# Four first columns of q and k through the SyncE and ScalarE queues instead of three

## The chip, the cores and the metric

The kernel runs on one core of one Trainium2 chip. Its time is the device time of one execution in microseconds (us); the median of five runs is given. The engines are PE (matmul, with PEld for its weight loads), DVE (vector), ACT (scalar), POOL and SP. Transfers between memory (HBM) and the core's SBUF go through 16 DMA engines, which serve several queues: SP and ACT each issue into a hardware queue (in the profile q1 and q10), POOL into a software queue (q0). A transfer in POOL's queue can convert fp32 to bf16 on its way; one in the other two keeps the type.

## What is computed

A cross-covariance attention is followed by a mixture of adapters. With B = 4 batches, N = 6400 rows and C = 256 channels:

```python
def _attn_ref(q, k, v, tau):
    qn = q / (np.linalg.norm(q, axis=1, keepdims=True) + 1e-06)
    kn = k / (np.linalg.norm(k, axis=1, keepdims=True) + 1e-06)
    s = kn.transpose(0, 2, 1) @ qn / tau
    s = s - s.max(-1, keepdims=True)
    a = np.exp(s)
    a /= a.sum(-1, keepdims=True) + 1e-09
    return v @ a

def _moe_ref(x, w_gate, A, B):          # x: the attention's output, 25600 x 256; 8 experts of rank 16, the best 2 of each row
    topk = np.argpartition(-(x @ w_gate), 2, axis=1)[:, :2]
    ...
    delta[mask] += w[mask, k, None] * ((x[mask] @ A[e]) @ B[e])
    ...
    return x + delta
```

The inputs q, k and v are fp32, 26.2 MB each; the output is fp32, 26.2 MB. For the first step of each batch, all of q and k has to pass through the 256 x 256 product before any row of v can be used.

## The kernel before

**Tiles.** The 6400 rows of a batch are split over 128 partitions, so that each partition holds 50 neighbouring rows. One such row on all partitions is called a column: 128 x 256 elements, 128 KB in fp32, contiguous within a partition. A batch has `NC` = 50 columns. q and k are loaded in pieces of 17, 17 and 16 columns (`QK`, L215) into bf16 tiles named `qk`, v in five pieces of 10 columns (`V`). For each column, step `G` (L571 to L589) multiplies k by q into the PSUM tile `acc` (L577, two matmuls of 256 columns), and, where the squared norms are not taken elsewhere, k by k (L581) and q by q (L586). For the column groups listed in `OFF` the squares are made on ACT (L599) and added up on DVE (L605) instead, so `G` has only its two matmuls there. Group 0, which is columns 0 to 5 of batch 0, is in `OFF` for q and for k.

**Order.** A planner written in Python (`Plan`, L69) simulates the engines with estimated costs, a model of PE's clock and a model of the DMA queues, and lists all steps in the order in which they would start. The program is then written out in that order; each engine works its own instructions strictly in this order, and waits where data is not there yet. Where the planner expects PE to be idle it can put filler matmuls (`warm`, L761), which write to an otherwise unused bank. POOL issues the loads of q, k and v in the planner's order (L562). At most eight of them are out at a time in the planner's model. SP issues the stores of the output (L912); some of these wait for a later load by way of a tiny transfer (`hold`, L629).

**The start.** For batch 0 the first piece of q and of k is loaded in two parts: `PARTS[(0, 0)]` is `((0, 2), (2, 15))`. The first part does not go through POOL. SP loads it for q and ACT for k, as fp32, into one scratch tile (`W["first"]`, in the buffer of the output tile y0, room for 10 columns), and these two instructions are moved ahead of everything else in the program (`first_ahead`, L428). ACT then casts each to bf16 into the `qk` tile (`do_cast`, L757). How many columns this first part holds is not taken from `PARTS` but from the constant `FIRST`, 3 here; POOL's load of the second part begins behind it:

```python
            if (b, c) == (0, 0):
                n = FIRST
                ...
                lo = "qk".index(what) * n
                W[what] = W["first"][:, lo:lo + n, :]
                early.append((nc.sync if what == "q" else nc.scalar).dma_start(W[what], src[b, :, 0:n, :]))
                return
        if (what, b, i) in (("q", 0, 0), ("k", 0, 0)):
            c, n = FIRST, c + n - FIRST
        nc.gpsimd.dma_start(t[:, c - c0:c - c0 + n, :], src[b, :, c:c + n, :])
```

The planner does not read `FIRST`. Behind the two first loads SP and ACT load the small constants (expert matrices and gate, L492 to L496), which DVE copies at 34.4 us (L538). The remaining pieces of q and k for batch 0 follow in POOL's queue, then the rest in the order of `WORDS`.

Of the kernel before, what the change touches and what calls it, by code (L numbers as in the profile page):

```python
# [32 lines left out]
class Clock:  # L33


    WINDOW, FIRST, LOW, HIGH = 3.413, 0.31, 0.5, 0.8

# [3 lines left out]
    def at(self, t):  # L41
        w = max(0, int((t - self.FIRST) / self.WINDOW) + 1)
        while len(self.cold) <= w:
            share = self.busy[-1] / self.WINDOW
            self.cold.append(share < (self.HIGH if self.cold[-1] else self.LOW))
            self.busy.append(0.0)
        return w

    def took(self, t, us):

        end, w = t, self.at(t)
        while us > 1e-9:
            pace = 2.0 if self.cold[w] else 1.0
            step = min(us * pace, max(self.FIRST + w * self.WINDOW - end, 1e-6))
            self.busy[w] += step
# [5 lines left out]
    def idle(self, t):  # L61

        w = self.at(t)
        return t - self.FIRST - (w - 1) * self.WINDOW - self.busy[w] > self.SPARE

# [347 lines left out]
PARTS = {(0, 0): ((0, 2), (2, 15)), (0, 2): ((34, 8), (42, 5), (47, 3)), (3, 2): ((34, 8), (42, 5),  # L413
        (47, 3))}
FINE = 2
FIRST = 3
OFF = {(0, 0, 'k'), (0, 0, 'q'), (0, 1, 'q'), (0, 2, 'k'), (0, 2, 'q'), (0, 4, 'q'), (0, 5, 'q'),
        (0, 6, 'k'), (0, 6, 'q'), (0, 7, 'k'), (0, 8, 'q'), (1, 0, 'k'), (1, 0, 'q'), (1, 1, 'q'),
        (1, 2, 'k'), (1, 5, 'q'), (1, 6, 'k'), (1, 7, 'k'), (1, 7, 'q'), (1, 8, 'q'), (2, 0, 'q'),
# [23 lines left out]
def kernel(  # L443
# [101 lines left out]
    def do_load(s, what, b, i, c, n):  # L545
        if what == "v":
            t, src, c0 = sb(s, "v", (b, i), [P, PC * max(n for _, n in V), C], BF16), v_v, c
        else:
            t = sb(s, "qk", (what, b, i), [P, max(n for _, n in QK), C], BF16)
            src, c0 = {"q": q_v, "k": k_v}[what], QK[i][0]  # L550
            if (b, c) == (0, 0):
                n = FIRST
                if "first" not in W:
# [6 lines left out]
# [3 lines that stand above are left out]
# [407 lines left out]
```

## Time and profile before

| | us |
|---|---|
| median of five runs | 255.23 (255.10 to 255.43) |
| the profiled execution, whole | 255.7 |
| its span, from the first to the last instruction | 253.9 |
| PE sees its first matmul | 5.6 |
| POOL's first load of q issued, landed | 1.4, 10.3 |
| POOL's first load of k issued, landed | 2.1, 14.6 |
| the last loads end, about | 223 |
| the last store issued, landed | 245.9, 253.0 |

The profile is a page about one execution. Its parts that are used here: the busy time of each engine; the span in 40 equal slices, where each digit is a busy share in tenths; the DMA queues with packets, MB and their time as a share of 16 engines; and the chain that ended last, followed back from the last instruction to whatever released each step. The trace behind it can be asked for instructions in order of time (start, duration, engine, line, operation, tile, shapes, and in brackets the idle time before it with what ended it), and for sums over chosen stretches. MB and GB/s count bytes as they are written: a transfer of POOL's that converts reads twice as many as are shown.

### The profile page before, as it was taken

What the parts mean: (1) busy time and instruction counts of PE and PEld (TensorE: products, weight loads), DVE (VectorE), ACT (ScalarE), POOL (GpSimd) and SP (SyncE); (2) the same over time, 40 slices, a digit from 0 to 9 for tenths busy, and PEclk for the clock granted to TensorE, in tenths of its full rate; (3) what the DMA queues carried; (4) which work ended last, traced back from release to release, by engine and by line L of the source; (5) the groups of instructions that cost most, each with busy time, mean ns of one, the idle gap of its engine ahead of it and who ended that gap; (6) DMA issues with size and microseconds to landing.
All of it is one profiled execution on the core that took longest, in us unless ns stands there. A gap on an engine that the chain in (4) does not pass through costs nothing.

```text
span 253.9 us, 5843 instructions
## 1 busy us (share of the span) xinstructions
PE 218.3 (86%) x2343; PEld 193.0 (76%) x2343; DVE 193.1 (76%) x527; ACT 149.5 (59%) x270; POOL 29.9 (12%) x58
## 2 busy tenths in 40 slices
PE   1165984899999998999999999989999989999960
PEld 0053962698989996799889989779999869999950
DVE  0055589779989987898999994689888889888810
ACT  4354437447767554877667538443766747557760
POOL 7001220040020002000030100510000200000000
PEclk9999997599999999999999999999999999999996
DMA  8999999999999999999999999999999999999994
GB/s 220 209 218 209 210 219 212 215 221 213 218 213 212 313 293 296 260 214 216 214 217 219 213 216 219 211 209 346 283 286 318 333 326 313 324 416 434 423 410 176
DMA packets 11819, 66.57 MB, mean 262 GB/s; under 512 B 1424, under 2 KB 2320, under 8 KB 7184
## 3 DMA queue, kind: packets, MB, share of 16 engines
q0 software_dynamic: 7488, 38.93, 74.7%
q1 hardware_dynamic: 3968, 26.74, 25.9%
q10 hardware_dynamic: 336, 0.53, 0.6%
q8 instruction: 18, 0.29, 0.4%
q14 instruction: 9, 0.07, 0.1%
HBM read 78.91 MB, written 26.21 MB: 414 GB/s over the span
## 4 chain that ended last, share of the span: by engine, by line
PE 53%; DMA 36%; DVE 3%; ACT 2%; POOL 1%; issue 1%; POOLq 0%; ACTq 0%
DMA qk<-in_k_dram 28%; PE Y_ps L899 13%; PE acc L577 9%; DMA qk<-in_q_dram 9%; PE T_ps L772 6%; PE Y_ps L904 6%; PE ZL_ps L796 4%; PE gzT_ps L886 4%; PE acc L586 2%; PE acc L581 2%; PE Z_ps L863 2%; DVE a_bf L747 2%; ACT a_exp L699 1%; PE log_ps L810 1%; POOL qk L562 1%
## 5 line engine op out<-in xcount | busy, mean ns | idle before, releaser
L577 PE MATMUL acc<-qk 128*128 128x256 bf16 x400 | 71.3, 286 | 18.7 <-DMA qk<-in_k_dram 12.5
L605 DVE TENSOR_TENSOR ssq<-ssq,sq 128x1280 f32<-128x1280 f32 (+1 forms) x27 | 43.4, 1606 | 23.2 <-ACT sq L599 21.1
L899 PE MATMUL Y_ps<-a_bf,vT 128*128 128x256 bf16 x400 | 60.0, 273 | 0.0
L753 ACT COPY y<-Y_ps 128x512 f32<-128x512 f32 x79 | 45.9, 586 | 18.3 <-PE Y_ps L904 15.6
L577 PEld LDWEIGHTS <-qk 128*128 128x128 bf16 x400 | 34.8, 102 | 23.9 <-DMA qk<-in_k_dram 15.2
L599 ACT ACTIVATE sq<-qk 128x1280 f32<-128x1280 bf16 (+1 forms) x27 | 36.9, 1366 | 26.6 <-DVE ssq L605 19.7
L899 PEld LDWEIGHTS <-vT 128*128 128x128 bf16 x400 | 38.9, 98 | 4.0
L904 PE MATMUL Y_ps<-ball,gzT 128*128 128x256 bf16 x200 | 38.2, 273 | 0.3 <-DVE gzT L755 0.3
L581 PE MATMUL acc<-qk 128*128 128x128 bf16 x242 | 34.4, 224 | 0.0
L772 PE MATMUL T_ps<-ident,v 128*128 128x128 f32 x200 | 27.3, 279 | 0.1
L562 POOL DMA_DIRECT2D v<-in_v_dram x20 | 12.1, 606 | 128.4 <-PE T_ps L772 81.0
L581 PEld LDWEIGHTS <-qk 128*128 128x128 bf16 x242 | 24.3, 100 | 3.4
L753 ACT COPY vT<-T_ps 128x512 f32<-128x512 f32 (+1 forms) x44 | 21.7, 515 | 8.2 <-PE T_ps L772 7.9
L874 DVE TENSOR_TENSOR gz<-zl,gateg 128x256 bf16<-128x256 f32 x70 | 26.0, 444 | 0.3
L772 PEld LDWEIGHTS T_ps<-ident,v 128*128 128x128 f32 x200 | 22.9, 145 | 1.1 <-issue 0.8
L586 PE MATMUL acc<-qk 128*128 128x128 bf16 x168 | 23.0, 218 | 0.0
L904 PEld LDWEIGHTS <-gzT 128*128 128x128 bf16 x200 | 19.4, 98 | 3.0 <-DVE gzT L755 0.6
L796 PE MATMUL ZL_ps<-waA_sb,vT 128*128 128x136 bf16 x280 | 19.7, 222 | 1.1 <-DVE waA_sb L741 0.9
L886 PE MATMUL gzT_ps<-ident,gz 128*128 128x128 f32 x100 | 20.4, 278 | 0.0
L796 PEld LDWEIGHTS <-vT 128*128 128x128 bf16 x280 | 17.8, 98 | 1.8 <-issue 1.5
L755 DVE COPY gzT<-gzT_ps 128x256 f32<-128x256 f32 (+1 forms) x39 | 14.9, 390 | 4.1 <-PE gzT_ps L886 3.6
L599 ACT ACTIVATE ssq<-qk 128x1536 f32<-128x1536 bf16 x8 | 11.9, 1483 | 10.1 <-DMA qk<-in_q_dram 5.3
(80 smaller groups left out, 271.0 us busy)
## 6 DMA issues: line engine op xcount, KB each, us to landing
out_dram<-y SPq DMA_DIRECT2D x18, 1280.0 KB, 17.9
v<-in_v_dram POOLq DMA_DIRECT2D x20, 640.0 KB, 20.3
qk<-in_q_dram POOLq DMA_DIRECT2D x7, 1088.0 KB, 23.5
qk<-in_k_dram POOLq DMA_DIRECT2D x7, 1088.0 KB, 28.2
qk<-in_q_dram POOLq DMA_DIRECT2D x2, 1024.0 KB, 18.1
qk<-in_k_dram POOLq DMA_DIRECT2D x2, 1024.0 KB, 22.4
out_dram<-y SPq DMA_DIRECT2D x4, 512.0 KB, 7.5
qk<-in_q_dram POOLq DMA_DIRECT2D x2, 512.0 KB, 17.1
```

The lines of the kernel that those rows point to most:

```text
L577: nc.tensor.matmul(acc[ic][:, 0:256], kt[:, j, ic::CC], qt[:, j, :], start=c == 0, stop=False, skip_group_check=True)
L581: nc.tensor.matmul(acc[ic][:, 256:384], kt[:, j, ic::CC], kt[:, j, ic::CC], start=False, stop=False, skip_group_check=True)
L586: nc.tensor.matmul(acc[ic][:, 384:512], qt[:, j, ic * P:(ic + 1) * P], qt[:, j, ic * P:(ic + 1) * P], start=False, stop=c == NC - 1, skip_ ...
L599: nc.scalar.activation(out[:, 0:n, :], t[:, j:j + n, :], ACT.Square)
L605: nc.vector.tensor_tensor(out=t, in0=t, in1=held["sq", (w, b, g), ""][:, 0:n, :], op=OP.add)
L753: nc.scalar.copy(out, in_)
L772: nc.tensor.matmul(ps[:, j, :], vt[:, c + j, :].bitcast(FP32), W["ident32"], is_transpose=True, start=(j == 0), stop=(j == n - 1))
L796: nc.tensor.matmul(ps[:, j, :], vT_of(b, i, c + j)[:, :, ic], st[b]["waA"][:, ic, :], start=(j == 0 and ic == 0), stop=(j == n - 1 and ic ...
L874: nc.vector.tensor_tensor(out=pairs[:, h].rearrange("p c (e r) -> p c e r", e=E), in0=z[:, 2 * h:2 * h + 2, :].rearrange("p c (e r) -> p c ...
L886: nc.tensor.matmul(ps[:, j, :], pairs[:, j * P:(j + 1) * P], W["ident32"], is_transpose=True, start=(j == 0), stop=(j == n // 2 - 1))
L899: nc.tensor.matmul(ps[:, j, :], vT_of(b, i, c + j)[:, :, ic], st[b]["a"][:, ic, :], start=(j == 0 and ic == 0), stop=False, skip_group_che ...
L904: nc.tensor.matmul(ps[:, j, :], pair[:, :, j], W["B"], start=False, stop=(j == 1), skip_group_check=True)
```

## The change

One constant changes. SP's load of q and ACT's load of k at the start take four columns instead of three (512 KB each instead of 384), the two casts on ACT take 1024 elements per partition instead of 768, and POOL's first load of q and of k begin at column 4 and take 13 columns instead of 14 (832 KB of fp32 instead of 896). The scratch tile then holds 8 columns of its 10. The planner's result, and with it the number and order of instructions on every engine, is the same.

```diff
 PARTS = {(0, 0): ((0, 2), (2, 15)), (0, 2): ((34, 8), (42, 5), (47, 3)), (3, 2): ((34, 8), (42, 5),
         (47, 3))}
 FINE = 2
-FIRST = 3
+FIRST = 4
```

## The prediction

> **What bounds the kernel now.** I read the page's busy shares and 40 slices first, then the DMA queues, then the chain that ended last, then the start and the end closely.
>
> ```profile
> PE 218.3 (86%) x2343; PEld 193.0 (76%) x2343; DVE 193.1 (76%) x527; ACT 149.5 (59%) x270; POOL 29.9 (12%) x58
> ...
> DMA  8999999999999999999999999999999999999994
> ...
> q0 software_dynamic: 7488, 38.93, 74.7%
> q1 hardware_dynamic: 3968, 26.74, 25.9%
> ...
> HBM read 78.91 MB, written 26.21 MB: 414 GB/s over the span
> ```
>
> PE is the busiest engine, but the row to look at is DMA: 9 in every slice between the first and the last. The two big queues took 74.7% and 25.9% of the time of 16 engines, together the whole span. So the transfers are the bound, and the total is bytes over rate: 105.1 MB at 414 GB/s are 253.9 us, the span. This does not depend on PE's small waits as long as no queue runs dry.
>
> ```profile
> 3.69 21.22 DMA qk<-in_k_dram
> 24.91 0.28 issue
> 25.19 21.10 DMA qk<-in_k_dram
> 46.33 2.32 PE acc L577 x10
> ```
>
> These are lines of the chain that ended last, in order of time: up to 46.33 us it is two loads of 21 us each. Their issue took 0.5 us; the rest was spent in the queue behind other loads. A load that is issued 0.3 us later lands no later.
>
> **The change, part by part.** The instruction orders of the two kernels are the same on all engines; only the sizes of six differ: the two first loads, their two casts, and the two Pool loads behind them, which shrink from 14 columns to 13 (896 to 832 KB).
>
> (a) *The extra column on SP's and ACT's queues.* While the hardware queue of k ran alone, and while the software queue ran alone, the DMA view has:
>
> ```profile
> q10 hardware_dynamic: 69, 0.21, 104.4%
> ...
> q0 software_dynamic: 242, 1.62, 100.1%
> ```
>
> The first line is from 3.0 to 3.5 us: 69 packets of 3072 bytes, full engines, 0.21 MB in 0.5 us, 424 GB/s of fp32. The second is from 5 to 13 us: 1.62 MB written as bf16 in 8 us, 203 GB/s, which are 405 GB/s of fp32 read. One column of one tensor is 128 KB of fp32. By the hardware queue it takes 0.131 MB / 424 GB/s = 0.31 us, by the software queue 0.131 / 405 = 0.32 us. Two columns are added to the one (+0.62 us) and taken from the other (-0.65 us). The sum is -0.03 us, below what these rows resolve. I take 0.
>
> (b) *Whether the bytes cost the same at the very start.* The stretches show start and end, length, busy times of PE, PEld, DVE, ACT, POOL, granted clock, DMA share and GB/s:
>
> ```profile
> 0.90:1.40 0.50, 0.00 (x0) 0.00 (x0) 0.00 (x0) 0.00 (x0) 0.00 (x0) 1.00 0.78 129
> 1.40:1.90 0.50, 0.00 (x0) 0.00 (x0) 0.00 (x0) 0.09 (x1) 0.48 (x1) 1.00 1.18 154
> 1.90:2.40 0.50, 0.00 (x0) 0.00 (x0) 0.00 (x0) 0.50 (x1) 0.50 (x2) 1.00 0.69 215
> 2.40:2.90 0.50, 0.00 (x0) 0.00 (x0) 0.00 (x0) 0.50 (x1) 0.42 (x2) 1.00 0.95 375
> ```
>
> From 0.90 to 2.40 us only (129 + 154 + 215) x 0.5 = 0.249 MB moved, where 424 GB/s would have needed 0.59 us: 0.91 us are lost. If the slow part costs by packet and not by byte, a 4096-byte packet carries a third more in it, and the bytes added are free. All 0.26 MB free would be -0.65 us, the lower bound. If the loss grows with the size of q's first load, it is 0.91 x 1/3 = +0.30 us, the upper bound. The trace cannot tell which. From 2.40 us on the rate is near full, and most of the extra bytes move there, so I take 0, and keep -0.65 and +0.30.
>
> (c) *What becomes later at the start, and its cover.* q's and k's first loads were issued at 0.00 and 0.12 us and landed 3.5 and 4.6 us later, at 3.5 and 4.7: with 0.31 us for each column ahead of them they become 3.8 and 5.3. A cast of 768 elements took 0.82 us; two lengths of the squares (1.25 us for 1280 elements, 1.48 for 1536) give 0.23 us for 256 more, so 1.05 us. The two casts end at 6.4 instead of 5.54 us, and PE begins there. On PE, 6 matmuls took 1.46 us at the start; 8 take 1.95, until 8.4 us. On ACT the next instruction behind the casts is:
>
> ```profile
> 10.44 1.48 ACT L599 ACTIVATE ssq<-qk 128x1536 f32<-128x1536 bf16 x1 [4.90 <-DMA qk<-in_q_dram]
> ...
> 14.65 1.89 PE L577 MATMUL acc<-qk 128*128 128x256 bf16 x8 [7.60 <-DMA qk<-in_k_dram]
> ```
>
> ACT sat idle 4.90 us before its next work and PE 7.60 us, so 0.9 us more of casts costs nothing. Without this cover it would be 0.9 us.
>
> The constants behind these loads on the SP and ACT queues land 0.6 us later than at 5.6 us; the copies on DVE that read them begin at 34.4 us. Pool's q load (issued at 1.42, 8.9 us to landing, so 10.3) lands 0.62 later by the hardware bytes ahead of it and 0.32 earlier by its own: at 10.6 us. Pool's k load (2.07 and 12.5) stays at 14.6. So ACT's squares at 10.44 move to 10.75, their DVE add from 13.32 to 13.6, and Pool's ninth load, which waits for q's landing, is issued at 10.9 instead of 10.63. That load landed 24 us after its issue: its place in the queue is kept. All of these have their next wait at 14.6 us or later, on something unmoved.
>
> (d) *What PE is spared behind k's landing.* Column 3 now runs in the idle time before 14.65 us: 2 matmuls of 0.236 us. Its 14 columns become 13, and PE's next wait, for the load that lands at 24.91, begins earlier. Nothing is gained; PE waits longer. This touches the clock:
>
> ```profile
> 20.40:23.82 3.42, 1.58 (x11) 0.89 (x9) 1.87 (x2) 1.48 (x1) 0.53 (x1) 1.00 1.01 211
> ...
> 37.47:40.88 3.41, 1.00 (x8) 0.71 (x8) 3.31 (x13) 1.90 (x3) 0.00 (x0) 1.00 1.06 222
> 40.88:44.30 3.42, 1.96 (x6) 0.53 (x4) 3.32 (x5) 2.86 (x2) 0.00 (x0) 0.50 1.00 209
> ```
>
> The stretches are cut at the times at which the granted clock changed. After 1.00 us of PE work in 3.41 us the clock was halved (at 40.88); after 1.58 us it was kept (at 23.82). The 0.47 us spared are of slow matmuls (the clock became full only at 20.40, where they halve), so the 1.58 become 1.58 - 0.24 = 1.34 us, between the two. I take the clock as kept, and price the other case as a rival.
>
> The Trainium skill, TensorE: Matmul & The Clock Gate, Part 1, speaks against the change in one point: it says PE falls back to half its clock after at least one idle window of some 3.4 us, and the wait before 24.95 us grows from 2.98 to 3.2 us. By that rule the clock would be kept, for no window is wholly idle, and the edit costs 0. But the rows above show a halving after a window with 1.00 us of work in it, so here the measurement decides and the case stays open.
>
> **Sum.** Own time of the profiled execution: 255.7 us, 253.9 of span and 1.8 around it. Bytes 0, start 0 (-0.65 to +0.30), casts 0, PE 0. The median, 255.23, is 0.47 under that execution; the forecast stands on the median: 255.2 us. The likeliest case has 254.8 to 255.6.
>
> **Rivals.**
>
> *1. The start gives something (faster).* The added bytes ride in the slow 1.5 us for free. For it: q's packets there were few and slow with nothing else in the queues. Against: 0.249 of q's 0.39 MB had moved by its end; the rest and k's come later at full rate. Whole, -0.65: 254.6 us; it shows where Pool's first k load lands, now 14.6 us.
>
> *2. PE's clock falls at 23.82 us (slower).* Place: PE works from 24.95 to 30.64 us; at half clock it gets through half of the 5.69 us, so 2.85 us of work are left over, until a full window wakes it at 30.64. Cover: PE's waits behind it, 0.67 us before 34.09 and 2.41 before 39.93, together 3.08. It decides from the point where the work in the window falls under a bound somewhere between 1.00 and 1.58 us, and it costs only if column 49 then comes late for the norms on DVE and ACT (39.8 us) and if that reaches a load's issue. Price: 0 with the cover, 2.85 without, 258.1. I take 1.0, for part of the cover lies before the end of the columns: 256.2 us. Against it: loads wait 17 us and more in the queue, so PE's lateness hardly reaches the DMA engines.
>
> *3. PE wakes one window earlier (faster).* In 44.30 to 47.71 us PE worked 2.70 of 3.41 us and stayed at half clock. If the k load at 46.3 lands 0.1 us earlier, this is 2.8. Waking at 47.71 instead of 51.12 spares half of 3.41, 1.7 us: 253.5 us if PE bound the rest. It does not: the last store was issued at 245.90 and landed 7.1 us later, behind other stores, so PE's end is covered.
>
> *4. The change does nothing, since the planner costs none of it.* The sizes in the instruction orders exclude it; what remains is that it moves no time, which is the forecast.
>
> **How the numbers follow.** What a measurement can tell from no change is about 0.2%, 0.5 us. Chances: forecast 0.62 (same 0.85 of it, the rest halved: 0.53 same, 0.045 to each side); rival 1 0.13 (0.12 faster); rival 2 0.18 (0.16 slower, 0.02 same); rival 3 0.07 (0.06 faster). Faster 0.22, same 0.55, slower 0.23 with the rounding. The range reaches to the foot of rival 1, 254.5, and to the price taken for rival 2, 256.1.
>
> **What would show it.** Right: the first loads land 0.3 and 0.6 us later, Pool's first k load at 14.6 +- 0.2, DMA at 9 from slice 2 to 39, the same MB in all queues but 0.26 MB more in SP's and ACT's and 0.13 less in Pool's, and a halved clock only from 40.9 to 51.1 us. Step (b) is wrong if Pool's k load lands at under 14.3 or over 14.8; (c) if ACT's squares or PE wait for a cast after 10 us; (d) if the clock is halved at 23.8 us. The forecast as a whole is wrong if a DMA slice between falls under 9, or if the landings of the middle loads have moved by other than those of the first.

## The result and the profile after

The changed kernel took 254.80 us (median of 21 runs, 254.69 to 255.36) beside 255.41 us for the kernel before (39 runs, 255.08 to 255.91). The ratio is 0.9979, with a 95% interval of 0.9973 to 0.9985: 0.54 us faster, 0.38 to 0.69. This is just over the 0.2% that counted as a change, and inside the range, but it is not the forecast's 255.2 with no change.

The page of the changed kernel shows the same DMA-bound picture, with the bytes moved between the queues as foreseen:

```profile
span 253.1 us, 5843 instructions
...
DMA  9999999999999999999999999999999999999995
...
q0 software_dynamic: 7488, 38.80, 74.6%
q1 hardware_dynamic: 3968, 26.87, 26.1%
q10 hardware_dynamic: 336, 0.66, 0.8%
```

POOL's queue wrote 0.13 MB less of bf16 (0.26 of fp32 less to read), SP's and ACT's 0.13 MB more each. The DMA digits differ in the first slice, 9 for 8, and in the last, 5 for 4. The span is 0.8 us shorter, more than the medians differ: the profiled execution before took 255.7 us, 0.3 over its median of the 39 runs, and the one after took 254.87, 0.07 over its median.

The start in order of time (start, length, engine, line, in brackets the idle time before and what ended it):

```profile
4.14 1.04 ACT L758 CAST qk<-y 128x1024 bf16<-128x1024 f32 x1 [0.31 <-DMA y<-in_q_dram]
...
5.44 1.04 ACT L758 CAST qk<-y 128x1024 bf16<-128x1024 f32 x1 [0.26 <-DMA y<-in_k_dram]
...
6.54 1.89 PE L577 MATMUL acc<-qk 128*128 128x256 bf16 x8 [6.54 <-ACT qk L758]
...
10.04 1.48 ACT L599 ACTIVATE ssq<-qk 128x1536 f32<-128x1536 bf16 x1 [3.56 <-DMA qk<-in_q_dram]
...
13.95 1.46 PE L577 MATMUL acc<-qk 128*128 128x256 bf16 x6 [5.52 <-DMA qk<-in_k_dram]
```

Everything fed by SP and ACT comes later, everything fed by POOL earlier. The casts are 0.22 us longer and end 0.94 us later, and PE runs 8 matmuls for 6 at once, in time it has to spare. But the squares on ACT begin at 10.04 instead of 10.44, and PE's wait for POOL's k load ends at 13.95 instead of 14.65 us. From this second shift on the two traces keep a distance: POOL's next loads of 1088 KB take 15.9 and 20.5 us to their landing instead of 16.6 and 21.2. The chain that ended last, in order of time, goes through other loads, but has the same shape:

```profile
4.73 24.43 DMA qk<-in_k_dram
29.15 0.28 issue
29.44 21.93 DMA v<-in_v_dram
51.36 0.04 issue
51.41 0.67 PE T_ps L772 x4
```

It reaches PE's work only at 51 us, again by two loads whose time is spent in the queue, not in their issue.

### The profile page after: what moved, and what is told of

Read it like the earlier page. It is cut to its first block, busy times and chain, and to the rows that moved or that the text cites. A ratio compares the mean times of both kernels' runs of the same rounds, so it can differ in the third digit from the quotient of the medians.

```text
span 253.1 us, 5843 instructions
## 1 busy us (share of the span) xinstructions
PE 217.1 (86%) x2343; PEld 192.3 (76%) x2343; DVE 193.0 (76%) x527; ACT 150.5 (59%) x270; POOL 29.9 (12%) x58
## 4 chain that ended last, share of the span: by engine, by line
PE 50%; DMA 38%; DVE 4%; ACT 2%; POOL 2%; issue 1%; ACTq 0%; POOLq 0%
DMA qk<-in_k_dram 21%; PE Y_ps L899 13%; DMA v<-in_v_dram 9%; DMA qk<-in_q_dram 9%; PE acc L577 8%; PE Y_ps L904 6%; PE T_ps L772 6%; PE ZL_ps L796 4%; PE gzT_ps L886 4%; PE acc L586 2%; PE acc L581 2%; PE Z_ps L863 2%; DVE a_bf L747 2%; ACT a_exp L699 1%; PE log_ps L810 1%; POOL qk L562 1%
## 5 line engine op out<-in xcount | busy, mean ns | idle before, releaser
L599 ACT ACTIVATE sq<-qk 128x1280 f32<-128x1280 bf16 (+1 forms) x27 | 36.9, 1365 | 27.2 <-DVE ssq L605 19.7
L581 PE MATMUL acc<-qk 128*128 128x128 bf16 x242 | 34.7, 225 | 0.0
L772 PEld LDWEIGHTS T_ps<-ident,v 128*128 128x128 f32 x200 | 22.0, 141 | 2.8 <-DMA v<-in_v_dram 0.9
L586 PE MATMUL acc<-qk 128*128 128x128 bf16 x168 | 23.6, 223 | 0.0
L755 DVE COPY y<-Y_ps 128x512 f32<-128x512 f32 x21 | 14.3, 689 | 3.4 <-PE Y_ps L904 3.1
```

Of the source, the lines that this page charges most:

```text
L581: nc.tensor.matmul(acc[ic][:, 256:384], kt[:, j, ic::CC], kt[:, j, ic::CC], start=False, stop=False, skip_group_check=True)
L586: nc.tensor.matmul(acc[ic][:, 384:512], qt[:, j, ic * P:(ic + 1) * P], qt[:, j, ic * P:(ic + 1) * P], start=False, stop=c == NC - 1, skip_ ...
L599: nc.scalar.activation(out[:, 0:n, :], t[:, j:j + n, :], ACT.Square)
L755: nc.vector.tensor_copy(out, in_)
L772: nc.tensor.matmul(ps[:, j, :], vt[:, c + j, :].bitcast(FP32), W["ident32"], is_transpose=True, start=(j == 0), stop=(j == n - 1))
```

## The experiments

Three theories were set up. A: at the start the DMA engines get less done than later, and bytes that ride there are free. B: the gain is PE's, which has column 3 behind it early. C: a chance of the layout, the execution or PE's clock windows. D (POOL's packets come too early) and E (the constants' small packets should run beside POOL's and not alone) came up on the way. One quantity is compared throughout: the HBM traffic of the first 12.5 us, which is the MB of q1 and q10 plus twice those of q0 (POOL's queue writes half of what it reads). The DMA view of that stretch, before:

```profile
q0 software_dynamic: 243, 1.63, 66.0%
q1 hardware_dynamic: 416, 0.52, 17.7%
q10 hardware_dynamic: 336, 0.53, 12.9%
```

and after:

```profile
q0 software_dynamic: 252, 1.57, 60.9%
q1 hardware_dynamic: 416, 0.66, 19.8%
q10 hardware_dynamic: 336, 0.66, 16.0%
```

These are 4.31 and 4.46 MB. The rate later is about 0.43 MB a us (215 GB/s written by POOL's queue from 7.5 to 12.5 us before, twice that read), so 0.15 MB are 0.35 us; two traces of one kernel differ by 0.04 to 0.06 MB in it.

**Column 3 loaded twice** (`twice`):

```diff
-                n = FIRST
+                n = FIRST + 1
 ...
-        nc.scalar.copy(held["qk", (what, 0, 0), ""][:, 0:FIRST, :], W[what])
+        nc.scalar.copy(held["qk", (what, 0, 0), ""][:, 0:FIRST, :], W[what][:, 0:FIRST, :])
```

> SP and ACT load four columns, POOL still loads fourteen: column 3 of q and of k is loaded twice (once into the scratch tile, where nobody reads it), 0.26 MB of fp32 more in all. Theory A (the DMA engines are underfed in the first 6 us, and bytes that ride there are free): 0 to +0.15 us against before (ratio 1.000 to 1.0006), POOL's first k load lands at 14.5 to 14.8 us. Theory B (the gain is PE's, which has column 3 behind it before k lands, and bytes cost the same everywhere): +0.6 us, ratio 1.0024, landing at 15.2 us, and no gain from the four columns since PE still waits for POOL's part. Theory C (a chance of the program's layout or of PE's clock windows): no relation, within 0.5 us.

Measured: 255.33 against 255.25 us, ratio 1.0002 (0.9994 to 1.0011); POOL's first k load was issued at 2.1 us and took 12.5, so it landed at 14.6. 4.52 MB in 12.5 us, 4.26 without the bytes loaded twice:

```profile
q0 software_dynamic: 239, 1.60, 61.5%
q1 hardware_dynamic: 416, 0.66, 19.3%
q10 hardware_dynamic: 336, 0.66, 14.9%
...
qk<-in_k_dram POOLq DMA_DIRECT2D x1, 896.0 KB, 12.5
```

The added 0.26 MB, 0.6 us by the rate later, cost at most 0.3. A holds; B, which charged 0.6 us, falls.

**Column 3 not loaded** (`skip`):

```diff
-            c, n = FIRST, c + n - FIRST
+            c, n = FIRST + 1, c + n - FIRST - 1
 ...
+        nc.scalar.copy(held["qk", (what, 0, 0), ""][:, FIRST, :], W[what][:, FIRST - 1, :])
```

> SP and ACT load three columns, POOL begins at column 4: column 3 of q and of k is not loaded, ACT copies column 2 in its place (256 elements per partition, two copies of about 0.4 us). 0.26 MB of fp32 less in all. Theory A: bytes in POOL's queue cost in full, so -0.6 us against before, ratio 0.9976, the same as the changed kernel within 0.15 us; POOL's first k load lands at 13.9 to 14.1 us. Theory B: -0.6 us for the bytes and -0.5 for PE, ratio 0.9957. Theory C: no relation.

Measured: 254.48 us, ratio 0.9970 (0.9959 to 0.9980), -0.77 us (-0.51 to -1.05). The same column saved in POOL's queue gives about the whole gain of the change, as A had it in time. Its landing was missed: k landed at 14.7 us, not at 13.9 to 14.1, with 4.25 MB moved. The loads that landed by 30 us came no earlier than before either; the first that did were two of 320 KB, after 26.2 and 27.2 us instead of 27.2 and 28.3.

**Five columns, and two** (`f5`, `f2`): `FIRST = 5` and `FIRST = 2`.

> Five first columns by SP and ACT, twelve by POOL. Theory A: if the start still has room, another -0.3 to -0.65 us against the changed kernel (ratio to before 0.9954 to 0.9968), POOL's first k load at 13.3 to 13.6 us; if four columns filled it, the same as four (0.9979), k at 13.9. Theory B: another step as large as the first, 0.9958, with the landings unmoved. Theory C: no order between three, four and five.

Measured: 254.83 us, ratio 0.9984 (0.9975 to 0.9993), k at 13.9 us, 4.50 MB. This is A's second branch: four columns fill what there is.

> Two first columns by SP and ACT, fifteen by POOL. Theory A: the DMA engines run dry for a while before POOL's packets come, +0.5 to +0.8 us against before (ratio 1.002 to 1.003), POOL's first k load at 15.1 to 15.4 us. Theory B: +0.5 us with the landings unmoved. Theory C: no order.

Measured: 255.25 us, ratio 1.0005 (0.9993 to 1.0017), k at 15.0 us, 4.19 MB. A missed here: it expected 1.002 to 1.003 and a landing at 15.1 to 15.4 us. The start is worse by 0.4 us at k's landing, as A's direction has it, but the loss in time is not told apart from none. Between POOL's k landing at 15.0, 14.6, 13.9 and 13.9 us for two, three, four and five columns there is an order that C does not give.

**The kernel before and the changed one once more** (`f3`, `f4`), for second traces:

> The kernel before once more, for a second trace of its start. Theory A (POOL's first packets, 7168 bytes written, are held up on some DMA engines unless enough hardware bytes run beside them): again a software queue whose time from 5 to 10 us is well over that of full packets, POOL's first k load at 14.4 to 14.9 us, ratio 1.000 within 0.0008. If it lands at 13.9 to 14.2 with full packets, the 0.7 us seen between the two traces is a chance of one execution.

> The changed kernel once more, on the same chip as these three, for a second trace: 4.42 to 4.52 MB by 12.5 us, POOL's first k load at 13.8 to 14.1 us, ratio 0.9973 to 0.9985. If k lands at 14.5 us again, the shift seen in the first trace of it was chance.

Measured: `f3` 1.0005 (0.9996 to 1.0014), k at 14.6 us, 4.27 MB. `f4` 0.9978 (0.9969 to 0.9987), k at 14.0 us, 4.52 MB. The two pairs of traces agree, so a chance of one execution does not explain the shift.

What differs in POOL's first packets is seen from 5 to 7.5 us. First the kernel before, then the changed one:

```profile
q0 software_dynamic: 62, 0.44, 91.4%
q10 hardware_dynamic: 1, 0.00, 0.1%
```

```profile
q0 software_dynamic: 76, 0.51, 97.5%
q10 hardware_dynamic: 104, 0.05, 11.9%
q1 hardware_dynamic: 34, 0.01, 3.0%
```

Before, POOL's queue is alone there: 62 packets took 91.4% of 16 engines for 2.5 us, 590 ns each, where most packets of 14 columns took 549. After, 76 packets of 13 columns took 513 ns each, 512 being theirs; and the constants' small packets, 138 of them, run beside these instead of ahead. The single packets of the trace show where the 590 come from: 7 of POOL's first 16 packets took more than a tenth longer than 549 ns, up to 1146, and so did 12 of those that started from 5 to 7.5 us. There were gaps besides: from 7.5 to 12.5 us the same queue's packets came to 104.8% of 16 engines (packets overlap a little), not 91.4%. With two columns more packets are slow (672 ns each in this stretch, for packets that mostly took 587); with the column loaded twice almost none (553 of 549).

**Half of it** (`q4k3`): SP loads four columns of q, ACT still three of k (`FIRST` becomes a table by tensor).

> SP loads four columns of q, ACT three of k; POOL 13 of q and 14 of k. Theory A: half of the added bytes, so half of the gain or more: ratio 0.9985 to 0.9992, POOL's first k load at 14.1 to 14.4 us. Theory B (PE): column 3 still waits for POOL's k load, so no gain, 1.000.

Measured: ratio 0.9996 (0.9988 to 1.0005), k at 14.5 us, 4.39 MB. A missed: it expected 0.9985 to 0.9992 and a landing at 14.1 to 14.4 us. The MB are half way, the landing and the time hardly moved. 8 of POOL's first 16 packets were held up, as before (7). That k lands late because its slowest packets do is likely, but not shown.

**Other bytes at the start** (`fill`):

```diff
             if n_load == 2:
                 load_consts()
+                nc.sync.dma_start(W["first"][:, 6:8, :], v_v[3, :, 48:50, :])
```

> Three columns as before, and SP loads two columns of v of batch 3 into the unused part of the scratch tile, behind the adapters' constants; nobody reads them (0.26 MB of fp32 more in all). Theory A: the place of the added bytes at the start is what matters, not that they are q and k: free, ratio 1.000 to 1.0006, POOL's first k load at 14.4 to 14.8 us. If bytes cost the same everywhere: +0.6 us, ratio 1.0024, k at 15.2 us.

Measured: 256.25 us, ratio 1.0045 (1.0031 to 1.0059), k at 15.1 us. A's expectation failed: behind the constants the same 0.26 MB are not free, but cost what the rate says, +0.6, and more; 0.4 us of the rest lie behind the last store's landing, where the program end waits 1.3 us instead of 0.9. The added load landed at 10 us, so its packets run beside POOL's. What is free is not any byte near the start: those ahead of POOL's packets were, those beside them were not.

**POOL later** (`later3`):

```diff
             if n_load == 2:
                 load_consts()
-            if n_load == 4:
                 make_consts()
```

> Three columns as before; POOL makes the identity matrix (0.5 us of work) before its first load instead of after its second, so that its first two loads are issued some 0.5 us later and nothing else changes. Theory A: no bytes are added, the DMA engines run emptier: 0 to +0.5 us, ratio 1.000 to 1.002, POOL's first k load at 14.6 to 15.1 us. Theory D (POOL's packets are held up because they come too early, before about 5 us, whatever else runs): the hold-up is gone, -0.3 to -0.5 us, ratio 0.998 to 0.999, k at 14.1 to 14.3 us.

Measured: ratio 1.0002 (0.9993 to 1.0011), k at 14.7 us, 4.39 MB. POOL's first loads were issued only 0.2 us later, not 0.5, and POOL's first packet started at 4.42 us, no later than in the kernel before (4.50, and 4.55 in `f3`). D's gain did not come, but D was not tested: the packets did not move.

**The constants away from the start** (`late3`, `late4`, `late5`, with `FIRST` of 3, 4 and 5):

```diff
-        nc.scalar.dma_start(W["B0"], ...
+        nc.sync.dma_start(W["B0"], ...
 ...
-        nc.scalar.dma_start(W["wg0"], ...
+        nc.sync.dma_start(W["wg0"], ...
 ...
-            if n_load == 2:
+            if n_load == 4:
+                nc.sync.dma_start(scrap, held["qk", ("q", 0, 0), ""][0:1, 16, 0:16])
                 load_consts()
-            if n_load == 4:
                 make_consts()
```

> Three columns. The three small constant loads are taken from the start: all go to SP's queue behind a tiny transfer that waits for POOL's first q load (10.3 us). Theory A (POOL's first packets are held up unless hardware packets run beside them): POOL's packets now start alone after k's first load, as with two columns, so no gain: 4.15 to 4.35 MB of HBM traffic by 12.5 us (before: 4.31 and, in a second trace, 4.27; four columns: 4.46), ratio 1.000 to 1.001. Theory E (what four columns bring is that the constants' small packets run beside POOL's large ones and not alone): the gain comes without more columns, 4.42 to 4.5 MB, ratio 0.998.

> Four columns, and the constants late as in late3. Theory A: the hardware bytes beside POOL's first packets are fewer than with the constants there, so part of the gain is given back: 4.3 to 4.45 MB by 12.5 us, ratio 0.998 to 1.0. Theory E: as good as four columns or better, 4.45 to 4.55 MB, ratio 0.997 to 0.998.

> Five columns, and the constants late. By both theories k's first load reaches to about 5 us, where POOL's packets come: 4.45 to 4.55 MB by 12.5 us, ratio 0.997 to 0.9985. Much under 0.997 would be the best version of the case.

Measured: 1.0157 (1.0143 to 1.0171), 1.0181 (1.0162 to 1.0201) and 1.0186 (1.0169 to 1.0204), 4 us and more slower. The times answer another question, because the edit had a fault: ACT writes into the same small tile `scrap` that the tiny transfer fills, and waits for it. From the order of time of `late3`:

```profile
15.82 1.28 ACT L512 ACT_TABLE_LOAD   x1 [15.82 <-DMA scrap<-qk]
...
18.83 1.46 PE L577 MATMUL acc<-qk 128*128 128x256 bf16 x6 [18.83 <-ACT qk L758]
```

So PE began 13 us late, and the buffers came free late. The stretches of the same kernel (DMA share and GB/s at the end of each line) show what it costs:

```profile
131.00:132.00 1.00, 1.00 (x17) 0.97 (x15) 1.00 (x1) 0.93 (x2) 0.00 (x0) 1.00 0.69 138
132.00:133.00 1.00, 1.00 (x12) 0.74 (x10) 1.00 (x4) 1.00 (x4) 0.17 (x1) 1.00 0.21 41
133.00:134.00 1.00, 1.00 (x14) 0.93 (x13) 0.86 (x5) 1.00 (x1) 1.00 (x3) 1.00 0.03 5
```

The DMA engines ran dry for about 2 us at 131 to 134 us. Near there they do so in `late4` and `late5` too, and in no kernel outside these three. The first 12.5 us can still be read, for ACT's wait delays no load there: 4.36 MB with three columns, 4.32 with four and 4.56 with five. A expected 4.15 to 4.35 with three and 4.3 to 4.45 with four, E 4.42 to 4.5 and 4.45 to 4.55; with five both expected 4.45 to 4.55. Without the constants between them and POOL's packets, four columns gain nothing over three. That speaks against E, by one trace each.

**All together.** Taking off the bytes loaded for nothing and adding those left out, the useful MB in 12.5 us are 4.29 for three columns (mean of two traces), 4.49 for four, 4.50 for five, 4.19 for two, 4.26 for `twice`, 4.51 for `skip`, 4.39 for `q4k3` and `later3`, and 4.04 for `fill`. Divided by 0.43 MB a us, the differences to three columns are -0.47, -0.49, +0.23, +0.07, -0.51, -0.23 and +0.58 us. Measured were -0.54, -0.41, +0.13, +0.05, -0.77, -0.10 (`q4k3`), +0.05 (`later3`) and +1.15 us. All but `later3`, by 0.05, and `fill`, by its end, lie within their intervals (about 0.2 to 0.3 us to each side), `skip` at the edge of its own. Most of these MB are from one trace each, good to some 0.1 us, and the three late kernels are left out.

**When POOL's first packets are held up.** The single packets put all traces in one order. In the changed kernel, `f4`, `twice`, `fill` and `f5`, POOL's first packet starts at 4.93, 4.92, 5.00, 5.03 and 5.26 us, and its first 16 packets take their usual time, within 6 ns in the mean. In the nine others it starts at 3.64 (`late3`) to 4.79 us (`late5`), and the first 16 take 16% to 65% longer. `late4` is among these: four columns, but without the constants behind them, POOL starts at 4.11 us and 13 of the first 16 are held up. So the columns alone do not remove the hold-up. The order is the one that D would give, but a later start came with more hardware packets ahead or beside it, and no run moved POOL's start alone. What the packets before 7.5 us took beyond their usual time, spread over 16 engines, is 0.36 and 0.38 us in the two traces with three columns, 0.01 and 0.04 with four. By this estimate the hold-up is about two thirds of the gain. It is not all that counts: `fill` has no such packet, and moved no more in 12.5 us than the kernel before (4.30 MB, 0.26 of them useless).

## Why the prediction was partly right

**The bound: right.** Bytes over rate is what decides. No slice's DMA share fell, and what was won by 12.5 us was still there late in the run: the traffic up to 220 us by the same view is 92.45 MB before and 92.62 after.

**(a) The price of a column: right for the steady stream, wrong at the start.** It gave 0.31 us by one queue and 0.32 by the other. The second came from 5 to 13 us, 203 GB/s, and was taken for POOL's full rate. It was not: the same view later, from 14.5 to 23 us, has 1.82 MB in 8.5 us, 214 GB/s. The 5% between the two rows are 0.41 us lost within that stretch, about the size of what the change recovers, and they could be read beforehand. A row from the place of the change was used as a price, and not compared with the same row elsewhere. At 214 the column costs 0.31 us by either queue, so the sum of (a) stays near 0; what was missed is the loss beside it, which belongs to (b).

**(b) The start: the step that failed.** The forecast took 0 between -0.65 and +0.30; the runs showed -0.54 (-0.38 to -0.69), close to the lower bound. Rival 1, at 0.13, was the case that came, but not for its stated reason. It put the free ride into the slow 0.9 to 2.4 us of q's first load. Worked out from the single packets' starts, lengths and sizes, the traffic by 2.5 us was 0.304 and 0.291 MB in the two traces with three columns, 0.351 and 0.311 with four: two traces of one kernel differ by up to 0.04 there. By 5 us it was 1.18 and 1.18 against 1.30 and 1.30, by 7.5 us 2.12 and 2.11 against 2.29 and 2.30. So of the 0.18 MB gained by 7.5 us only 0.03 were there at 2.5. Most of the gain is made from 2.5 to 7.5 us, where the constants' small packets ran and where POOL's first packets were held up. That the range still held the result is in part luck: its lower bound, all 0.26 MB free, was argued from a stretch that gave little of it. Stretches of this part (DMA share and GB/s written at the end), before:

```profile
5.00:6.00 1.00, 0.41 (x3) 0.28 (x4) 0.00 (x0) 0.54 (x1) 1.00 (x3) 1.00 0.86 172
6.00:7.50 1.50, 1.05 (x5) 0.45 (x3) 0.00 (x0) 0.00 (x0) 0.34 (x1) 1.00 0.95 182
```

and after:

```profile
5.00:6.00 1.00, 0.00 (x0) 0.00 (x0) 0.00 (x0) 0.74 (x2) 1.00 (x3) 1.00 1.24 244
6.00:7.50 1.50, 0.96 (x5) 0.70 (x6) 0.00 (x0) 0.49 (x1) 0.34 (x1) 1.00 1.05 217
```

Before, POOL's queue starts at 172 and 182 GB/s; after, the first of these stretches carries hardware packets too, and the second, at 217, is at the steady rate.

**(c) What becomes later: right.** Casts of 1.04 us (1.05 worked out), ended at 6.48 (6.4), PE at 6.54 and 1.89 us for 8 matmuls (1.95), all covered. The first loads' landings were 0.3 and 0.1 us later than foreseen (4.1 and 5.4). Its landings of POOL's loads, 10.6 and 14.6, were wrong with (b): 10.0 and 13.9.

**(d) and rival 2, the clock: the mechanism came, the cost did not.** The granted clock in the changed kernel's trace, in stretches cut where it changed:

```profile
17.75:21.16 3.41, 2.36 (x21) 1.60 (x18) 1.89 (x2) 1.42 (x2) 0.53 (x1) 1.00 1.05 220
21.16:24.57 3.41, 0.29 (x3) 0.27 (x4) 1.76 (x1) 1.58 (x2) 0.05 (x1) 1.00 0.99 204
24.57:27.99 3.42, 3.42 (x27) 2.93 (x26) 1.49 (x1) 1.86 (x2) 1.00 (x2) 0.50 1.06 213
27.99:31.40 3.41, 3.41 (x45) 3.19 (x44) 1.76 (x1) 1.59 (x2) 0.94 (x2) 1.00 1.08 210
```

After a window with 0.29 us of PE work the clock was halved at 24.57 us, in the wait that rival 2 named (it had 23.82), and PE was at half speed until 27.99. The execution was none the slower: 254.87 us. In `f4` the clock was halved in the same place (24.64 to 28.05), in `f5` not before 39.60, and these took 254.69 and 254.70. The price with the cover, 0, was the right one; 1.0 was not. Why the window held so little is not what was argued. PE's clock was full from 17.75 us on instead of 20.40, so PE was done sooner and waited 4.17 us there, not 3.2; and the windows lie elsewhere. Their borders are at 20.40 and 23.82 us before and at 21.16 and 24.57 after, 0.75 us apart; in `f3`, the kernel before once more, the clock became full at 19.91. The Trainium skill, TensorE: Matmul & The Clock Gate, Part 1, says that the window runs freely and does not start with the kernel; the traces agree. Arguing from one trace's window borders to another kernel's was therefore idle.

**Rival 3** would have had PE's clock back sooner. In the changed kernel's trace it was halved from 45.05 to 48.47 us only, before from 40.88 to 51.12; the time moved by what the bytes say, so nothing shows a gain from it. (Of the chances, the 0.23 for slower is 0.025 more than its parts, 0.16 and 0.045.) That PE's time is covered holds for small amounts only: with PE 13 us late, the loads ran dry.

**Open.** Why POOL's first packets are held up in the traces where they start before 4.8 us, and not in those where they start at 4.92 us or later, was not found, nor whether the start itself or the hardware packets around it decide. The traces give no engine number with a packet, and no run delayed POOL's loads enough to tell.

## What to carry to other kernels

In a kernel that the DMA engines bound from start to end, look for time at its two ends: compare the rate of the first microseconds with the same row in the steady part, and try more bytes in the queue that starts first, until the second one's slow beginning is covered. Here four columns did it, and a fifth won nothing more; the same bytes beside the second queue's packets were paid in full. Check a price that is read at the place of the change against the same row elsewhere. And before an experiment moves a transfer, see which engine shares its tile, for a wait can land on an engine that was not meant.

## What was not expected of the hardware

- 0.26 MB more, put ahead of POOL's packets, took no measurable time (1.0002, 0.9994 to 1.0011); the same amount behind the constants took 0.6 us and more.
- POOL's packets of 13 and 14 columns took 512 and 549 ns mostly, but some of the first took up to 1.1 us more where POOL's first packet started before 4.8 us, and at most 0.16 us more where it started at 4.92 us or later. With these held-up packets goes a wider spread of the times: 255.08 to 255.91 us in 39 runs with three columns and 254.66 to 256.08 in 11 with two, against 254.64 to 254.95 in 11 with five and, but for one run of 255.36, 254.69 to 255.00 in 21 with four.
- The clock was halved after windows of 3.41 us that held 1.00 and 0.29 us of PE work, and kept after one with 1.58.
